# A new order of the same jobs, with fewer changes of the matmul engine's tiling, in an attention-plus-MLP kernel

## Chip, core and metric

The kernel runs on one core of one Trainium2 chip. The metric is the device time of the execution in microseconds; the shown time is the median of three runs. All engines of the core have their own queue of instructions and run them in the order in which they were written; they wait for each other by semaphores. PE is the matmul engine (PEld its loading of the stationary operand), ACT the scalar engine, DVE the vector engine, POOL the general one, SP the queue that issues most transfers.

## The reference

x is 2048 tokens of width 512. It is normalised once (xn), and three terms are added:

```
xn  = layernorm(x)
out = x + attention(xn) + mlp(xn)

attention: 32 heads of 16, 4 segments of 512 tokens
  q, k, v = xn @ wq, xn @ wk, xn @ wv
  per segment s and head:
    p     = softmax(q k^T * scale + causal mask);  a_dot = p v
    a_mem = phi(q) M / (phi(q) z + 1e-6)           phi(t) = t+1 if t>0 else exp(t)
    o     = g * a_mem + (1-g) * a_dot              g = sigmoid(beta)
    M    += phi(k)^T v ;  z += sum phi(k)
  o @ wo
mlp: y = layernorm(xn);  gelu(y @ w1 + b1) @ w2 + b2,  w1 is 512 x 1792
```

## The kernel before

Every weight and activation is carried as a high and a low float16 half, so that each product is three float16 matmuls (line 480, function split3). The work is cut into 1307 small jobs. A *unit* i (0 to 15) is one segment with 8 heads; j (0 to 15) is one half of the MLP's hidden width for 256 tokens.

| job | what it does | PE line, matmuls of one job | tiling of the PE array |
|---|---|---|---|
| T, V | project q, k (T) and v (V) | L480, 12 of 512 columns | whole (128 x 128) |
| D | first MLP product | L480, 12 of 256 columns | whole |
| out | output projection | L815, 12 of 512 | whole |
| warm | 8 matmuls whose result nobody reads | L828 | whole |
| M | logits for the row maximum | L621, 2 or 4 | two row halves (64 x 128) |
| R | turns the 32 row maxima, which go to DRAM (L641) and back (L644) as two more rows of qst | L499, 2 | row halves |
| S | logits again, transposed, with the maximum taken off; ACT makes the exponential (L666), POOL zeroes the masked part (L675) | L661, 2 or 4 | row halves |
| e | second MLP product | L797, 6 | row halves |
| Xt, N, Qd, ratio | turns and the memory's product | L499, L571, L427 | row halves |
| pv | p v and the sum of p for four heads | L690, 8 a block | four column strips (128 x 32) |
| K | memory update | L602 | column strips |

Others have no matmul: G and H are the gelu and its split (L763, L770 to L772, ACT and POOL), O makes the normalised output of a unit (L714, L540, L541, L545, L546, L720 to L726), Q the memory's quotient, X the layer norm, wl, wm and ws load a weight, square it (L311) and split it (L366 to L371); wf (L343, L345) sums the squares on PE for the scale with which a weight is split.

The order in which the jobs are written is a string, ORDER: each letter takes the next job of one of 28 streams (function streams), and a job issues its instructions on all engines at once, so the string sets every engine's order, and that of SP's transfers. A second string, BANKS, names the one of the eight PSUM banks for each call of dense() in that order. There is no scheduler behind it. For the table of ACT functions, plan() adds a load where gelu and exponential follow each other.

The PE array is used as one whole, as two halves by rows, or as four strips by columns. A *change of tiling* is a place in PE's order where a matmul of one kind follows one of another.

Of the kernel before, what the change touches and what calls it, by code (L numbers as in the profile page):

```python
# [56 lines left out]
def streams():  # L57
# [42 lines left out]


ORDER = (
    "aatcucuccvavtctveecttcetcuvaactvuvtaatcattavdtubcwwvccfwxxcxwxyxyxxgyhxcoxxvwxofooowcvwzyzoiyyiazgyyziiynzoiiys"
    "ppAnziiniicvzvcniiooAzmAihiiopzqqiqcivpqjpqjijqqijizqjiqqjiiAwszBzoAskkkkmjiAojoijsoAijAqjqjasAfoAopgkkkkpjpjqq"
    "jlpoolojjjooilihAAkkkkpaiqqiqijqjqqijqjiqjqjisBfgpiiqkkkkmpliqqiooiqpBlqoBopohijjiojiijpolsjiqaqajqiqiqqiiqapka"
    "kmkktspaqijqiqjqiqajqbqajopijjgBfopkkkBkjjjlooooBlhjjjolqiqqiipkkkkjiqqijqqjjiqiqjjqiqiqiBkkkkmpliilfnplimpngrr"
    "mrjjponijqjqjinjipiskmkkmkaiijrijjoojiqsjqqjiqiiiqqkkkkihlqlfmlogojqjqjqqjjasoojmkkkkmqjiqjqjjaojjpipmooisikkkk"
    "lpilhiofmgoooqiqpppqiqiqqqiiiqqpsosmoiqqiiqiqppsslooijqjojijojijoiaakkkkmpaijqjqjaqqqjiqqjiqjqiikmkkakbqiaqqahl"
    "olfqjjojqmjgjjoolmmkkkkmhjjoojjiitjiojiippkkkkliiilnfnimpligniinipmrrijjrsijqjqiqjiqjqiipkmkkksiqjqijqjqjiqjqii"
    "qjqikmpkkkiprlqsphlfojmjgopjjlojpjoomokmkkkqiqisjojiqisjqiqijqqijqhiqqiiqjsqiiqppmkkkkilalofomqpgopaoooospmlajq"  # L110
    "qqjqqjqjqiiqiqqqjqiqqipipooooiijooppoiaakkkkmajiqpisqqjiqjqjaiqaqhjqqqjqaaqmkkkkbjlfoljqjmjgojjqolmkkkkmmjjjooj"
    "jioijoiiippkpkkkiinliifniiilnnimlgrpmjjrmjjjrrijikkpskkiqqijqiqijqqjiqjiqjqiqjiqiispqkpkskksqilqoplfojmjgjjjpoo"
    "oojolmkkkkiqjiqpsjiqiqijqjqiqijqjiqiqiqiiqqkksmkpikplolfjjqmjgjjjoooooklpkmkkjiiopjqiqijqjiqpjqiqijqiqqiqiiqikk"
    "pspkkqiplpoooopljjjqqqjqjjqooolkpskmkpkmqqqpqjpjqqqjqjqpqqjqjqqqkmkkkqlllqqqqqqqqqrrrr"
)

BANKS = (
    "012345670123457063571265407321640573216405732164053271640527163054271630542713605427105472105427105472105472015"  # L120
    "470251407251405712470512470512470536124075631254076340125637123756123576132576132576132576132576135402761350427"
    "163054273106542736574326574326537425632754632574631072456310724563071245360712453620731620731067203617621073621"
    "073621073621037621037621037261702361475023671540263701524603175246031746013746013713460713471630471630463714067"
    "314056723410523674105236741052367410527410527410527410527410527140352671450326475103264751023674523674523647253"
    "647236547236475264735264107532410765324107265431067512043675120436751204736152047361520473615270346150312750317"
    "250317253107250371257013275027135027134650132754062751340621375460376054370567403056374065374065307645307645307"
    "642153076241076241076241076253410762534621075346210754316024310264310432610432610324610324612403246013752640163"
    "754207156437120564371205647312056473120564731206547321065473265104723607423460273460273642073642073642051736420"
    "157642031765420316750316705315631705630157630157630157306173504621357462017345620147536210436024136024316403216"
    "403216403216403216740536740536740536740536271406"  # L130
)


# [777 lines left out]
```

## Time and profile before

| | |
|---|---|
| median of 3 runs | 694.83 us (694.37 to 696.42) |
| profiled execution | span 693.1 us from first to last instruction; what lies around it is 1.7 us by the median, as no time of its own is listed for it |
| PE | 678.7 us busy, 98% of the span, 6359 matmuls |
| DVE, ACT, POOL | 535.4 (77%), 522.7 (75%), 347.2 us (50%) |
| PE idle before matmuls, by releaser | 9.5 us in all, of which 0.2 us between 35 and 680 us |
| transfers | 55.12 MB, mean 80 GB/s |

Matmuls are pipelined, and the recorded end of one is modelled and overlaps the next, so PE's busy time is no measure of useful work. The chain of waits and the distance from one start to the next tell more: a piece of the chain is the time by which the end moves on. PEld's idle time is marked "issue" where it waits for nothing that the profile shows.

### The profile page before, as it was taken

The numbers are of one execution on the slowest core, as the hardware profiler recorded it, in microseconds if no ns is written. First come the engines' busy times: TensorE is split into PE (matmuls) and PEld (weight loads), VectorE is DVE, ScalarE is ACT, GpSimd is POOL, SyncE is SP. The second block draws the span as 40 slices with busy tenths as digits, with TensorE's granted clock in tenths as the row PEclk, the third lists the DMA queues.
The fourth block names the chain that finished last, engine by engine and source line by source line (L and its number), as shares of the span: only waits on it lengthen the run. The fifth ranks groups of instructions, "written<-read, shape, count | busy, mean of one in ns | idle before, by whom it ended". The sixth has DMA issues, their size and how long they took to land.

```text
span 693.1 us, 16949 instructions
## 1 busy us (share of the span) xinstructions
PE 678.7 (98%) x6359; PEld 395.7 (57%) x6359; DVE 535.4 (77%) x1695; ACT 522.7 (75%) x1013; POOL 347.2 (50%) x533
## 2 busy tenths in 40 slices
PE   7799999999999999999999999999999999999997
PEld 6465556576654555566554456567564456656653
DVE  4499978897795887998798786888678595969442
ACT  5989898878795659857795697757795687778870
POOL 5276768365624425664334445454362546455752
PEclk9899999999999999999999999999999999999999
DMA  9984222420204213431113224231120416140101
GB/s 272 283 238 136 64 63 63 108 62 14 84 10 115 87 44 74 100 71 33 51 45 92 63 72 99 63 93 33 31 80 24 132 18 152 18 108 3 18 1 61
DMA packets 51790, 55.12 MB, mean 80 GB/s; under 512 B 4782, under 2 KB 40636, under 8 KB 51708
## 3 DMA queue, kind: packets, MB, share of 16 engines
q1 hardware_dynamic: 49404, 49.84, 25.3%
q0 software_dynamic: 2304, 4.20, 3.7%
q8 instruction: 50, 0.82, 0.5%
q14 instruction: 32, 0.26, 0.1%
HBM read 36.99 MB, written 17.04 MB: 78 GB/s over the span
## 4 chain that ended last, share of the span: by engine, by line
PE 78%; ACT 10%; POOL 4%; DVE 3%; issue 2%; DMA 1%; SPq 1%; POOLq 0%; ACTq 0%; DVEq 0%
PE ps L480 33%; PE ps L797 16%; PE ps L690 10%; PE ps L815 6%; PE ps L661 5%; PE ps L621 5%; ACT pt L666 2%; DVE ps L628 2%; PE ps L571 2%; PE ps L499 1%; ACT hT L763 1%; ACT hT L771 1%; SPq L252 1%; POOL w1s L371 1%; DMA pt<-in_A_wk_dram 1%
## 5 line engine op out<-in xcount | busy, mean ns | idle before, releaser
L628 DVE CUSTOM_DVE_ANT_0 ps<-ps,mask 128x512 f32<-128x512 f32 (+3 forms) x512 | 233.8, 522 | 16.1 <-PE ps L621 14.9
L666 ACT ACTIVATE pt<-ps,qkcs 128x512 f32<-128x512 f32 (+1 forms) x384 | 206.1, 624 | 35.3 <-PE ps L661 33.5
L797 PE MATMUL ps<-w2s,hT 64*128 64x512 f16 x1344 | 176.7, 376 | 0.2
L480 PE MATMUL ps<-xnT,w1s 128*128 128x256 f16 x1344 | 157.8, 273 | 0.0
L675 POOL TENSOR_SCALAR_AFFINE_SELECT pt<-pt 128x256 f32<-128x256 f32 x256 | 99.1, 414 | 92.0 <-ACT pt L666 91.0
L480 PEld LDWEIGHTS <-w1s 128*128 128x128 f16 x1344 | 127.3, 98 | 29.1 <-issue 11.3
L772 POOL TENSOR_TENSOR hT<-hh,hT 128x512 f16<-128x512 f32 x64 | 67.8, 1059 | 82.8 <-ACT hT L771 81.0
L797 PEld LDWEIGHTS <-hT 64*128 64x128 f16 x1344 | 76.3, 94 | 50.7 <-issue 6.0
L690 PE MATMUL ps<-pt,vt 128*32 128x512 f32 (+3 forms) x1024 | 77.3, 435 | 0.1
L756 DVE SCALAR_TENSOR_TENSOR hT<-ps,sc,sr 128x256 f32<-128x256 f32 x112 | 52.1, 478 | 27.2 <-PE ps L480 27.0
L628 DVE DVE_READ_ACCUMULATOR2_ANT mc<- 128x1 f32 x512 | 70.6, 138 | 0.0
L661 PE MATMUL ps<-qst,kst 50*128 50x512 f16 (+3 forms) x512 | 67.5, 298 | 0.3 <-ACT pt L666 0.2
L621 PE MATMUL ps<-kst,qst 48*128 48x256 f16 (+3 forms) x512 | 67.1, 297 | 0.5
L771 ACT ACTIVATE hT<-hh 128x512 f16<-128x512 f32 x64 | 36.6, 572 | 33.4 <-POOL hh L770 32.9
L690 PEld LDWEIGHTS ps<-pt,vt 128*32 128x32 f32 x1024 | 31.3, 109 | 42.4 <-issue 30.8
L770 POOL TENSOR_SCALAR hh<-hT,sc 128x512 f32<-128x512 f32 x64 | 41.8, 653 | 26.6 <-ACT hT L763 24.9
L720 POOL TENSOR_TENSOR nN<-nN,oT 128x512 f32<-128x512 f32 x16 | 20.3, 1267 | 61.3 <-DVE oT L546 61.3
L763 ACT ACTIVATE hT<-hT,b1t 128x256 f32<-128x256 f32 x112 | 46.4, 495 | 0.2
L480 PE MATMUL ps<-xnT,wqs 128*128 128x512 f16 x192 | 45.6, 389 | 0.0
L480 PE MATMUL ps<-xnT,wks 128*128 128x512 f16 x192 | 44.3, 379 | 0.0
L480 PE MATMUL ps<-wvs,xnT 128*128 128x512 f16 x192 | 44.0, 380 | 0.1
L815 PE MATMUL ps<-wos,oT 128*128 128x512 f16 x192 | 43.2, 380 | 0.6 <-POOL oT L726 0.6
(217 smaller groups left out, 890.0 us busy)
## 6 DMA issues: line engine op xcount, KB each, us to landing
kd<-hl SPq DMA_DIRECT2D x48, 128.0 KB
qd<-hl SPq DMA_DIRECT2D x48, 128.0 KB
kst<-kd SPq DMA_DIRECT2D x32, 192.0 KB
qst<-qd SPq DMA_DIRECT2D x32, 192.0 KB
acc<-in_A_x_dram SPq DMA_DIRECT2D x16, 256.0 KB
acc<-in_B_b_dram POOLq DMA_DIRECT2D x16, 256.0 KB, 4.1
out_dram<-acc SPq DMA_DIRECT2D x16, 256.0 KB
xt<-in_A_x_dram SPq DMA_DIRECT2D x14, 256.0 KB
```

Source lines behind the costliest of these rows:

```text
L480: T.matmul(p, wsl(ws, k, a), xsl(xs, k, b), start=s0 and i == 0, stop=s1 and i == 3 * n - 1)
L621: T.matmul(p[:, o:o + n], stk[i, 0][r, t, P * qb:P * qb + P], stk[i, 1][r, t, :n], start=True, stop=True)
L628: V.tensor_tensor_reduce(p[:, o:o + n], p[:, o:o + n], mask[:, 512 - n:], 1.0, -3e38, OP.add, OP.max, mc[:, 16 * b + 4 * t + qb:16 * b + 4 ...
L661: T.matmul(p[:, o:o + n], stk[i, 1][r, t, P * kb:P * kb + P], stk[i, 0][r, t, P * kb:], start=True, stop=True)
L666: A.activation(e[:, OFF[kbs[0]]:OFF[kbs[0]] + o], p[:, :o], AF.Exp, scale=qkcs[:, 1, i % NG:i % NG + 1])
L675: G.affine_select(v, v, pattern=[[0, 2], [1, P]], compare_op=OP.is_ge, fill=0.0, base=0, channel_multiplier=-1)
L690: T.matmul(p[32 * c:32 * c + 32, P * kb:], vt[s, kb][:, 4 * g + c, 16 * odd:16 * odd + 32], pt[i, 2 * c + odd][:, OFF[kb]:OFF[kb] + LEN[kb ...
L756: V.scalar_tensor_tensor(hz[:, fi, :], p[:, :256], col(F1 + fh), srow[hs][:, own], op0=OP.mult, op1=OP.mult)
L763: A.activation(z, z, AF.Gelu_apprx_tanh, bias=b1t[:, FH * (j % 2) + f:FH * (j % 2) + f + 1])
L772: G.tensor_tensor(hT[:, z, 1, :], t, hT[:, z, 0, :], op=OP.subtract)
L797: w = T.matmul(pes[j][a], hTs[fh][r, fi, u, P * a:P * a + P], w2s[r, fo, v, :], start=n == 0 and m == 0, stop=fi == FH - 1 and m == 2, ski ...
L815: T.matmul(p, o[:, u, P * b:P * b + P], wos[:, g, v, :], start=i == 0, stop=i == 3 * NG - 1)
```

## The change

The two strings are replaced. Every stream gives the same jobs in its own order, each job issues the same instructions, and the 32 later loads of ACT's function table stay 32. What differs is how the streams are interleaved, and the bank of each job. In PE's order the whole array is visited 68 times instead of 90, the strips 32 times instead of 34, and the row halves 89 times instead of 110; so there are 189 changes of tiling instead of 234.

```diff
 ORDER = (
-    "aatcucuccvavtctveecttcetcuvaactvuvtaatcattavdtubcwwvccfwxxcxwxyxyxxgyhxcoxxvwxofooowcvwzyzoiyyiazgyyziiynzoiiys"
...
-    "pspkkqiplpoooopljjjqqqjqjjqooolkpskmkpkmqqqpqjpjqqqjqjqpqqjqjqqqkmkkkqlllqqqqqqqqqrrrr"
+    "atttatccauutactavccectuaccvvccuvtvtvevwteavbwawvtucwvwwfxcgxdxhtxcyxccwxvgxsxcfxoxyooxoyyoiiyzynziiyyzitoczoyz"
...
+    "kkkkpqsiplospooqjljqqjqqjljjqooookkkppkqpjqqqpjjqqqqqjjqqjmqkpkkqqmqqqqlqqqqqqllqrrrr"
 )
...
 BANKS = (
-    "012345670123457063571265407321640573216405732164053271640527163054271630542713605427105472105427105472105472015"
...
+    "012345670123457062134570216345270163452071634502751634702516340725163407256134072134207103714203712403174203174"
...
 )
```

**First place: the end of unit 6, PE.** Before, from the fourth product of MLP part 7 (D, L480 with w1s) to its last; ps_n is a PSUM tile. Loads of the stationary operand and repeats of a row are left out.

```order
L480 MATMUL ps_4655<-xnT,w1s 128x256
...
L621 MATMUL ps_4669<-kst_92,qst_90 128x512
...
L661 MATMUL ps_4677<-qst_89,kst_91 128x512
...
L797 MATMUL ps_4413<-w2s,hT_116 128x512
...
L661 MATMUL ps_4691<-qst_89,kst_91 128x384
...
L480 MATMUL ps_4701<-xnT,w1s 128x256
...
L661 MATMUL ps_4715<-qst_89,kst_91 128x256
...
L621 MATMUL ps_4723<-kst_92,qst_90 128x384
...
L480 MATMUL ps_4741<-xnT,w1s 128x256
...
L661 MATMUL ps_4755<-qst_89,kst_91 128x384
...
L480 MATMUL ps_4779<-xnT,w1s 128x256
```

The same jobs now:

```order
L797 MATMUL ps_4456<-w2s,hT_116 128x512
...
L661 MATMUL ps_4713<-qst_89,kst_91 128x512
...
L661 MATMUL ps_4719<-qst_89,kst_91 128x384
...
L480 MATMUL ps_4729<-xnT,w1s 128x256
...
L480 MATMUL ps_4743<-xnT,w1s 128x256
...
L480 MATMUL ps_4757<-xnT,w1s 128x256
...
L480 MATMUL ps_4771<-xnT,w1s 128x256
...
L480 MATMUL ps_4785<-xnT,w1s 128x256
...
L661 MATMUL ps_4799<-qst_89,kst_91 128x256
```

Five products D stand together; before, M, S and e (row halves) stood between them, and the array changed its tiling six times in this stretch, now twice.

**Second place: unit 7's row maxima, PE.** R (L499 with mc) sends the maxima off; S (L661 with qst_90) is the first that needs them back. Before:

```order
L499 MATMUL ps_5087<-ident,mc 96x64
...
L499 MATMUL ps_5098<-ident,xt 128x64
...
L797 MATMUL ps_4894<-w2s,hT_115 128x512
...
L499 MATMUL ps_5124<-ident,xt 128x64
...
L499 MATMUL ps_5139<-ident,phk 128x64
...
L480 MATMUL ps_5155<-xnT,w1s 128x256
...
L480 MATMUL ps_5173<-xnT,wks 128x512
...
L797 MATMUL ps_4894<-w2s,hT_115 128x512
...
L661 MATMUL ps_5204<-qst_90,kst_92 128x512
```

Now:

```order
L499 MATMUL ps_5081<-ident,mc 96x64
...
L427 MATMUL ps_5093<-ident,rat 128x64
...
L797 MATMUL ps_4876<-w2s,hT_115 128x512
...
L661 MATMUL ps_5111<-qst_89,kst_91 128x256
...
L499 MATMUL ps_5119<-ident,xt 128x64
...
L499 MATMUL ps_5133<-ident,xt 128x64
...
L797 MATMUL ps_4876<-w2s,hT_115 128x512
...
L690 MATMUL ps_5155<-pt,vt_85 32x512 x4
...
L661 MATMUL ps_5176<-qst_90,kst_92 128x512
```

A projection and a product D between the two have gone elsewhere, and a block of pv has come in.

**Third place: the start, PE.** From the first projection (wks) to the first product with w1s. Before:

```order
L480 MATMUL ps_393<-xnT,wks 128x512
...
L343 MATMUL ps_416<-am,ones 128x1 x2
L343 MATMUL ps_431<-am,ones 128x1 x2
L345 MATMUL ps_431<-am,ones 128x1
L480 LDWEIGHTS wqs
L480 MATMUL ps_453<-xnT,wqs 128x512
...
L343 MATMUL ps_476<-am,ones 128x1 x2
L499 MATMUL ps_486<-ident,phk 128x64
...
L480 MATMUL ps_504<-xnT,w1s 128x256
```

Now:

```order
L480 MATMUL ps_390<-xnT,wks 128x512
...
L480 MATMUL ps_415<-xnT,wqs 128x512
...
L840 MATMUL ps_439<-ident,mhl 128x14
L499 MATMUL ps_451<-ident,phk 128x64
...
L343 MATMUL ps_472<-am,ones 128x1 x2
L345 MATMUL ps_472<-am,ones 128x1
L480 LDWEIGHTS wqs
L480 MATMUL ps_502<-xnT,wqs 128x512
...
L480 MATMUL ps_529<-xnT,wks 128x512
...
L480 MATMUL ps_559<-xnT,w1s 128x256
```

Unit 0's second projection stands ahead of the sum of w1's squares (ps_431 before, ps_472 now), both projections of unit 1 stand ahead of the first product with w1s, and the sum for w2 (ps_476) has gone behind four such products. On ACT and SP the jobs of the start follow the same new string.

More of the change, by code (lines that the diff above doesn't have):

```diff
@@ L102 @@
 ORDER = (
-    "aatcucuccvavtctveecttcetcuvaactvuvtaatcattavdtubcwwvccfwxxcxwxyxyxxgyhxcoxxvwxofooowcvwzyzoiyyiazgyyziiynzoiiys"
[L104 to L112, printed above, removed]
@@ L113 @@
-    "oojolmkkkkiqjiqpsjiqiqijqjqiqijqjiqiqiqiiqqkksmkpikplolfjjqmjgjjjoooooklpkmkkjiiopjqiqijqjiqpjqiqijqiqqiqiiqikk"
-    "pspkkqiplpoooopljjjqqqjqjjqooolkpskmkpkmqqqpqjpjqqqjqjqpqqjqjqqqkmkkkqlllqqqqqqqqqrrrr"
+    "atttatccauautactavccectuaccvvccuvtvtvevwteavbwawvtucwvwwfxcgxdxhtxcyxccwxvgxsxcfxoxyooxoyyoiiyzynziiyyzitoczoyz"
+    "ypiiisznniwipzAiizozApsnooiiAApqiqiocAcviqivjqpqsjqjqjqijqiqjqBziimzkkkBkisqjzqijoijqhjAoijAAjAfgAoopkskpkkjpBl"
+    "pjloooooAojqjaiAqsiqjqqjlpiqiimkkkkiiqjqqjijqqjiqjhqajqifgopiikkpkmkaiholotplosjijojijpoijioaaqpliaqjqipqpiqiqa"
@@ new lines @@
+    "qkkmkkqajqiqijqijqaqbiqpajBoijjfBBgpomkkBakkjjljooloohjilqiqjiqqjiqipikBkkkijqqijqqjiqiiqjqjqiqjmikkkklomfljjjg"
+    "nlpnannjijriijkkkmpkpijirjisapirrjimqjqjqiiqjqsiikpskkkhlliqqmlofgjqqjqqjqjqqjjommkkkkjiioojijojijosojipimkkkpk"
+    "oloilhimfoogooospipiqpiqqilqsmqqqiiqqiiopoijqipqjqiqjiqpspjjooooojpiakkkkmqisaqjiaqqhjaqamiqjqjqjqiqqqibqjaaqkk"
+    "kkjjlljofjmjgojklkmkkmjjoojjjooijikkppkkiiinlpomipiinnlihilmiifpgprrpimrnjpiqiqjqiqjiqjjrjikkpkkmiiqjisqjqiqjiq"
+    "ijqjqiqhmqjikkkkllsafmjjgopmosoloooojjqijqqjqiimkkkkjmiqqiqshqijiqjqijqjqiiqjqiikkppkkolpolfimpgopoomoojjlqqaqj"
@@ L115 @@
+    "qjqiasqqijqipsqipqqjpiqqipqioooooooiapakkkaksmijqjaajqqiqjqqjqjiqsbqiaaqikkmkklfljqqjqqjmjjgojklkkkjjjoooomhijj"
+    "ooiijkpkmkkiliipnmniippiniliiflnmigmrrjsjjrjjqiqqjiiqmqikkkpkijqqijqijqijqjqiqjsiqipikkpkkqirlplfmjjgoooomjmjjo"
+    "ooilijkkkpkijqipqqjiqsjqjiqiqjiqiqjqipiqikkkkpqilossplfqjmqpgoljjosjjjookkmkkjpjmioijojiqijqijpqiqiqqiiqpiqqiqi"
+    "kkkkpqsiplospooqjljqqjqqjljjqooookkkppkqpjqqqpjjqqqqqjjqqjmqkpkkkqqmqqqqlqqqqqqllqrrrr"
 )
 BANKS = (
-    "012345670123457063571265407321640573216405732164053271640527163054271630542713605427105472105427105472105472015"
@@ L121 @@
[L121 to L130, printed above, removed]
+    "012345670123457062134570216345270163452071634502751634702516340725163407256134072134207103714203712403174203174"
@@ new lines @@
+    "230174203170432157064321570643215706342157630157613057163057160537610537160751360751342607513426730541267304512"
+    "763041527630145276307652307652305726350735260375261740523461705234671056273410562374256374256374256347235467325"
+    "462573426571304265710426357014263750142016375204175632017456302173402713247013240173240127401237405162374052136"
+    "740532617405236147052361470523614705236147052367052367052367053267052367052145213647052136475036475306475347534"
+    "076534076534076213450762145360275314602715346027315426703154267103542671035647210356472103564721305172305172305"
@@ new lines @@
+    "173205132705312573015273027153207153624071254073612540736125346125346125314261543261452365124356132540761325407"
+    "613254076312546315241653241624160752341607523416075342160342136402136241036241036214036271536420736154250734612"
+    "507613245074561327045613270456132047561320475613204756132041732041732041372041307420713402713402713456027156023"
+    "471560234761502135476210365210356231506231503612503612503612503472560134725360147021543670251647356145673145673"
+    "145673145673145670312470371240371240371240536712"
```

## Prediction

> **What bounds the kernel now.** I read the page's busy shares first, then who waited for whom on PE, then stretches of the span, then the chain of waits.
>
> ```profile
> span 693.1 us, 16949 instructions
> PE 678.7 (98%) x6359; PEld 395.7 (57%) x6359; DVE 535.4 (77%) x1695; ACT 522.7 (75%) x1013; POOL 347.2 (50%) x533
> ...
> PE ps L343 <- ACT w1s L311: 4.5, 2, 3.3
> PE ps L828 <- POOL ones L171: 1.6, 1, 1.6
> PE ps L326 <- ACT wqs L311: 1.3, 1, 1.3
> PE ps L466 <- POOL xt L413: 1.0, 1, 1.0
> PE ps L815 <- POOL oT L726: 0.6, 1, 0.6
> PE ps L343 <- ACT w2s L311: 0.3, 1, 0.3
> PE ps L661 <- ACT pt L666: 0.2, 1, 0.2
> ```
>
> PE's idle time is 9.5 us in all, nearly all of it at the start; one 0.6 stands at the end, and between them 0.2. So PE's own stream sets the end. The other engines (stretches: us, then busy time of PE, PEld, DVE, ACT, POOL, then PE's clock):
>
> ```profile
> 20.00:25.00 5.00, 2.59 (x14) 1.44 (x12) 2.89 (x15) 4.94 (x10) 1.80 (x2) 0.97 1.10 345
> 25.00:30.00 5.00, 2.82 (x10) 1.91 (x11) 2.04 (x9) 4.75 (x10) 0.12 (x1) 0.50 1.11 343
> 30.00:35.00 5.00, 4.69 (x32) 2.82 (x31) 1.07 (x3) 4.97 (x10) 2.98 (x4) 0.84 0.46 137
> 40.00:90.00 50.00, 49.50 (x469) 29.26 (x468) 47.35 (x173) 44.74 (x89) 34.30 (x44) 1.00 0.48 136
> 90.00:660.00 570.00, 569.47 (x5463) 330.29 (x5463) 456.56 (x1440) 433.98 (x837) 283.42 (x441) 1.00 0.25 65
> ```
>
> Before 35 us ACT is the full engine, from 40 to 90 DVE and ACT are almost as full as PE, and from 90 on PE alone is: DVE has 113 of 570 us free, ACT 136. A saving on PE is worth its full size there, as long as the others hand over in time.
>
> **What a change of tiling costs.** The chain of waits in order of time (start, how far the end moved on, what):
>
> ```profile
> 303.38 2.73 PE ps L480 x24
> 306.11 0.32 PE ps L621 x2
> 306.43 0.22 PE ps L661 x2
> 306.65 0.65 PE ps L797 x6
> 307.52 1.42 PE ps L480 x12
> 313.93 2.29 PE ps L690 x32
> 345.44 0.48 PE ps L602 x32
> 345.92 2.15 PE ps L690 x32
> 580.38 5.35 PE ps L480 x48
> 615.05 6.66 PE ps L480 x60
> ```
>
> These L480 pieces are products D. Twelve cost 1.42, 24 cost 2.73, 48 cost 5.35, 60 cost 6.66: 1.31 for each dozen and 0.11 once, for coming from the row halves into the whole array. Back again: two 512-column matmuls on the row halves cost 0.32 right behind a D and 0.22 behind their like, so 0.10. Into the strips: 32 matmuls of pv cost 2.29 when they are first there, 2.15 when a memory update (L602) has gone in ahead of them, so 0.14. I take 0.10 for each change, with 0.09 and 0.14 as bounds.
>
> ```profile
> PEld L480 <- issue: 22.8, 77, 0.8
> ```
>
> This row shows why: the load ahead of an L480 stood idle 77 times for 22.8 us with no semaphore to wait for, 0.3 each, about as often as PE enters the whole array (90 visits). Within a run the load lies under the matmul before it; at a change it doesn't. [...]
>
> **The terms.** (1) 234 to 189 is 45 changes: 45 x 0.10 = **-4.5 us** (bounds 45 x 0.09 = -4.0 and 45 x 0.14 = -6.3). Nearly all lie behind 35 us, where no other engine covers them. The matmuls, the ACT table loads and all DVE, ACT and POOL work are the same in number and size.
>
> (2) The start. PE (start, busy, group, idle before it) and one row of ACT:
>
> ```profile
> 1.59 6.69 PE L828 MATMUL ps<-ones 128*128 128x256 f16 x48 [1.59 <-POOL ones L171]
> 28.64 4.18 PE L480 MATMUL ps<-xnT,wqs 128*128 128x512 f16 x12
> 33.25 0.38 PE L343 MATMUL ps<-am,ones 128*128 128x1 f32 x2 [0.31 <-ACT w2s L311]
> 33.96 2.79 PE L480 MATMUL ps<-xnT,w1s 128*128 128x256 f16 x24
> ...
> 30.90 0.61 ACT L370 ACTIVATE w1s<-w1s 128x512 f16<-128x512 f32 x1
> ```
>
> Today the sum of w1's squares holds PE until 28.64 us, and the projection behind it takes 4.18 us at half clock. The new order does that projection first, but puts about six more pieces like the 0.61 of ACT (four splits, two copies of projections) ahead of those squares. So the sum ends 3.6 us later, near 32.3; two projections of 2.6 follow (12 matmuls of 0.22, as the 37 in 8.16 under (4)), and the first w1s product starts near 37.7. What is "level"? Ahead of that product two projections are added (5.2) and the w2 sum is taken away (0.6), one change fewer: 33.96 + 4.5 = 38.5. I take 0 for the start, between -1.5 and, for one more stretch of half clock (6.8 us of it above, which lose 3.4), +3.4.
>
> (3) Hand-overs. Fewer visits mean longer runs, and with the same jobs some pairs stand closer. The closest and longest way is from R to S, through DRAM (chain, unit 13):
>
> ```profile
> 570.33 1.40 DMA md<-mhl
> ...
> 571.75 0.27 SPq L644
> 572.06 3.46 DMA qst<-md
> ...
> PEld L661 <- DMA qst<-md: 0.8, 2, 0.4
> PEld ps L690 <- POOL pt L675: 3.1, 11, 0.5
> ```
>
> That is 5.1 us from the write's issue to the read's landing, after ACT and DVE have emptied the turned maxima. Adding up PE's work between R and S in both orders (a D 1.31, an e 0.65, a pv block 2.18, and so on): under 5.5 us there are three units before and eight now; unit 7 falls from 6.8 to 4.5. It waited twice for 0.4 before. Between the last masked block and its pv less than 2.3 us of PE's work stand 4 times before, 10 times now; such loads waited 11 times for 0.28 each, though mostly under PE's own work. I take **+1.0** (2 of the waits of 0.4 more, and a little for pv), from 0 to +5.0: eight waits of 0.4 are 3.2, six of 0.3 are 1.8. The banks I put at nothing: the shortest way from a bank's last write to its next is 0.3 us of PE's work before and 0.4 now.
>
> (4) The end.
>
> ```profile
> 671.15 6.89 PE L797 MATMUL ps<-w2s,hT 64*128 64x512 f16 x60
> 677.97 2.61 PE L815 MATMUL ps<-wos,oT 128*128 128x512 f16 x11
> 681.20 8.16 PE L815 MATMUL ps<-wos,oT 128*128 128x512 f16 x37 [0.63 <-POOL oT L726]
> ...
> 671.02 0.69 DVE L546 SCALAR_TENSOR_TENSOR rc<-rc,rt 128x512 f32<-128x512 f32 x1
> 673.07 0.72 DVE L714 STREAM_SHUFFLE oT<-nD 128x512 f32<-128x512 f32 x1
> ```
>
> The last pv ends at 671.15, the twelfth matmul of the output projection can start at 681.20: 10.05 us, which ten e (6.5) and eleven matmuls (2.4) cover but for 0.85, from 680.35. Now 13 e cover 8.5 + 2.4 = 10.9, but two DVE instructions of the memory's quotient (0.69 each) have gone in ahead of the shuffle: 11.4. A shortfall of 0.5 is left: **-0.3**.
>
> Sum: -4.5 + 0 + 1.0 - 0.3 = -3.8. On the profiled execution the span goes from 693.1 to 689.3; what lies around it (1.7) doesn't change, so the median goes from 694.83 to **691.0 us**. A measurement of this kernel tells a change from none from about 0.3% on, 2.1 us: faster is under 692.7, slower over 696.9.
>
> **The rivals.**
>
> *The gain is handed back (about 695).* PE waits where it had 0.2 us of waits: the upper bound of (3), 5.0 in place of 1.0, gives 695.0. For it: the eight short ways from R to S, and from 40 to 90 us DVE with 2.65 of 50 us to spare, so that a block that comes late stays late. Against it: the shortest way from R to S was 4.4 us before (unit 14) and is 4.5 now, so no unit is asked for more than one was. [...]
>
> *The start loses the clock (slower, 697.8).* Now the first six warm-up jobs (the 48 matmuls of the L828 row) still end at 8.3 us; the first turn of x then waits for POOL's normalised tile, near 11 us, and the next sum waits for six squares on ACT, to about 17.5. Before, 2.59 us of work in 20 to 25 were too little, and the clock went to 0.50. If that happens twice, around 11 us and again around 25, with the projections in it, 2 x 3.4 = 6.8 us are lost: 691.0 + 6.8 = 697.8. It decides at the first w1s product: with the 4.5 us of changes still to be saved behind it, the whole is level when it starts at 43, and slower by 2.1 past 45. Against it: each of these gaps is near 2.7 us by my estimate from the pieces of ACT and POOL, where before two waits of 4.5 together, the longer 3.3, came close behind each other (the L343 row above), and 43 is 5 us behind what ACT's pieces give. [...]
>
> *Everything falls well (689).* No added hand-over waits, and the start gains 1: 691.0 - 1.0 - 1.0 = 689.0. For it: ACT's pieces put the first w1s product 0.8 ahead of level, and 113 of DVE's 570 us behind 90 us are free.
>
> **How the numbers follow.** Forecast 0.54, everything well 0.12, handed back or half price 0.24, slow start 0.10. Faster by over 0.3%: 0.54 + 0.12 = 0.66; within: 0.24; slower: 0.10. The range goes from 688.8 (all well) to 695.0 (handed back); it leaves out the slow start and the edges, about 2 in 10.
>
> **What would show it.** Right: in the chain D pieces still at 1.31 a dozen plus 0.11; PE's waits between 35 and 680 us under 1.5 us; the first w1s product between 36 and 40 us. Wrong: (1), if pieces on the row halves cost more than now where they aren't behind a change; (2), if that product starts past 41, or the clock row shows under 1.00 after 15 us for longer than before; (3), if PE's wait for qst, or its loads' for pt, grows by more than 2 us; (4), if PE idles over 1 us ahead of the last output projection. Past 694 the forecast is wrong, and past 697 its sign.

## The result and the profile after

The new order takes 721.5 us (median of 4 runs, 718.9 to 722.7) against 694.9 us of the old one measured beside it: 1.0375 times the time, 95% interval 1.035 to 1.040. It is 26.5 us slower; the forecast was 3.8 us faster, and the range ended at 695.0. The profiled execution is the shortest of the four (718.9 us, span 717.2), so its profile shows 24.1 us of the 26.5. Intervals leave out single executions in a slower state, of which two stand far off (860.9 us with short row maxima in the new order, 2413.3 us with everything left out).

The page of the new order; its last row is the share of each engine in the chain of waits:

```profile
span 717.2 us, 16987 instructions
PE 684.1 (95%) x6359; PEld 399.2 (56%) x6359; DVE 542.6 (76%) x1695; ACT 524.6 (73%) x1014; POOL 351.0 (49%) x533
...
PE 53%; DVE 15%; DMA 14%; ACT 11%; issue 4%; POOL 2%; SPq 1%; DVEq 0%; ACTq 0%; POOLq 0%
```

The work is the same, instruction for instruction, but for one load of ACT's function table more (1.28 us at 61.2 us, ahead of L851), so the later loads are 33 and not 32. Only 53% of the chain is PE's now; it was 78% before. DVE needs 542.6 us for the 1695 instructions that took 535.4. PE's waits between 35 and 680 us (total, times, longest), where there were 0.2 us before:

```profile
PE ps L661 <- DMA qst<-md: 6.9, 6, 3.4
PE ps L621 <- DMA qst<-qd: 4.2, 8, 0.9
PE ps L797 <- DVE hT L756: 1.7, 2, 1.3
PE ps L621 <- DVE mc L628: 1.2, 2, 0.8
PE ps L499 <- DVE mc L628: 1.1, 1, 1.1
PE ps L480 <- DVE w1s L367: 0.9, 1, 0.9
```

The two longest are the trips through DRAM: the maxima (md) and q (qd) that come back into qst. In the other four a matmul waits for a bank or an operand that DVE hands over late. They are spread over the run; the stretches that the prediction used (us, busy time of PE, PEld, DVE, ACT, POOL, PE's clock, DMA):

```profile
40.00:90.00 50.00, 46.52 (x429) 27.79 (x429) 45.93 (x167) 44.12 (x86) 33.04 (x40) 1.00 0.58 158
90.00:660.00 570.00, 552.96 (x5256) 321.43 (x5257) 449.11 (x1410) 417.79 (x806) 272.36 (x424) 0.99 0.24 64
396.90:403.70 6.80, 6.21 (x35) 3.00 (x37) 3.05 (x13) 3.05 (x5) 1.64 (x3) 0.50 0.13 42
```

From 90 to 660 us PE had 0.5 us without work before, and has 17.0 now. The last row is a stretch of half clock in the middle of the run, which the old order doesn't have.

How the delays of several queues add up can be followed at unit 8. The rows are of timelines (start, busy, what, idle time before) of POOL, DVE, PE, ACT and SP, with two pieces of the chain of waits (PE's x24, DMA) and one row of SP's waits:

```profile
374.18 1.16 POOL L772 TENSOR_TENSOR hT<-hh,hT 128x512 f16<-128x512 f32 x1 [0.74 <-ACT hT L771]
...
374.24 1.64 DVE L545 TENSOR_TENSOR oT<-oT,nD 128x512 f32<-128x512 f32 x1
...
377.07 0.65 PE L621 MATMUL ps<-kst,qst 48*128 48x384 f16 x5 [0.82 <-DVE mc L628]
378.10 0.38 PE L480 MATMUL ps<-xnT,wks 128*128 128x512 f16 x1 [0.38 <-DVE mc L628]
...
378.10 5.35 PE ps L480 x24
...
385.96 2.90 ACT L763 ACTIVATE hT<-hT,b1t 128x256 f32<-128x256 f32 x7
...
389.52 0.34 DVE L639 SCALAR_TENSOR_TENSOR mhl<-ps,mhl 32x64 f16<-32x64 f32 x2
392.22 0.69 DVE L545 TENSOR_TENSOR rc<-rc,rt 128x512 f32<-128x512 f32 x1 [2.36 <-ACT rt L541]
...
SPq L527 <- DMA qd<-hl: 1.7, 1, 1.7
...
390.71 0.79 SPq L527 DMA_DIRECT2D qst<-qd x2
391.56 0.91 SPq L737 DMA_DIRECT2D out_dram<-acc  x2
392.51 0.46 SPq L641 DMA_DIRECT2D md<-mhl  x1
...
392.51 3.40 DMA md<-mhl
...
397.49 1.02 PE L661 MATMUL ps<-qst,kst 50*128 50x512 f16 x2 [3.39 <-DMA qst<-md]
```

A product of DVE (L545) that lasts 0.69 us at 392.22 takes 1.64, beginning while POOL's L772 runs. The row maxima behind it end 0.95 late, so M and the two projections T of unit 9 start late on PE (0.82 and 0.38). Behind the projections, ACT has seven gelu pieces to do, and only then come unit 8's maxima; DVE has them ready at 389.86. On SP, unit 9's q must land first (1.7 us of waiting) and is fetched again (L527), and two rows of the output leave (L737), before the maxima's write is issued at 392.51, 2.65 us after they were ready. The write, issued behind these transfers, takes 3.40 us; it took 1.40 in unit 13 of the old order. PE stands still for 3.39 us, and its clock is at 0.50 for 6.8 us from 396.87 on, which by estimate costs another 3.1 (half of the 6.2 us that PE is busy in that stretch).

### The profile page after: what moved, and what is told of

Same layout as the page of the kernel before. It is cut to its first block, busy times and chain, and to the rows that moved or that the text cites. A ratio compares the mean times of both kernels' runs of the same rounds, so it can differ in the third digit from the quotient of the medians.

```text
span 717.2 us, 16987 instructions
## 1 busy us (share of the span) xinstructions
PE 684.1 (95%) x6359; PEld 399.2 (56%) x6359; DVE 542.6 (76%) x1695; ACT 524.6 (73%) x1014; POOL 351.0 (49%) x533
## 4 chain that ended last, share of the span: by engine, by line
PE 53%; DVE 15%; DMA 14%; ACT 11%; issue 4%; POOL 2%; SPq 1%; DVEq 0%; ACTq 0%; POOLq 0%
PE ps L480 16%; PE ps L797 15%; PE ps L690 6%; DVE ps L628 5%; PE ps L661 4%; PE ps L621 4%; PE ps L815 4%; DMA qd<-hl 4%; DMA qst<-qd 3%; DMA md<-mhl 2%; ACT hT L763 2%; DMA qst<-md 1%; ACT pt L666 1%; DVE hl L518 1%; DVE mc L628 1%
## 5 line engine op out<-in xcount | busy, mean ns | idle before, releaser
L628 DVE CUSTOM_DVE_ANT_0 ps<-ps,mask 128x512 f32<-128x512 f32 (+3 forms) x512 | 234.8, 522 | 18.7 <-PE ps L621 15.6
L797 PE MATMUL ps<-w2s,hT 64*128 64x512 f16 x1344 | 182.8, 379 | 1.8 <-DVE hT L756 1.7
L675 POOL TENSOR_SCALAR_AFFINE_SELECT pt<-pt 128x256 f32<-128x256 f32 x256 | 101.8, 422 | 116.3 <-ACT pt L666 115.2
L480 PE MATMUL ps<-xnT,w1s 128*128 128x256 f16 x1344 | 155.9, 273 | 1.3 <-DVE w1s L367 0.9
L480 PEld LDWEIGHTS <-w1s 128*128 128x128 f16 x1344 | 128.8, 98 | 27.5 <-issue 8.2
L797 PEld LDWEIGHTS <-hT 64*128 64x128 f16 x1344 | 78.7, 95 | 55.9 <-issue 8.2
L772 POOL TENSOR_TENSOR hT<-hh,hT 128x512 f16<-128x512 f32 x64 | 66.8, 1044 | 80.5 <-ACT hT L771 77.0
L621 PE MATMUL ps<-kst,qst 48*128 48x384 f16 (+3 forms) x512 | 74.2, 300 | 6.5 <-DMA qst<-qd 4.2
L661 PE MATMUL ps<-qst,kst 50*128 50x512 f16 (+3 forms) x512 | 72.6, 299 | 8.0 <-DMA qst<-md 6.9
L756 DVE SCALAR_TENSOR_TENSOR hT<-ps,sc,sr 128x256 f32<-128x256 f32 x112 | 51.3, 477 | 30.4 <-PE ps L480 30.3
L628 DVE DVE_READ_ACCUMULATOR2_ANT mc<- 128x1 f32 x512 | 71.3, 139 | 0.2
L661 PEld LDWEIGHTS <-kst 50*128 50x128 f16 x512 | 29.3, 95 | 38.7 <-issue 11.9
L621 PEld LDWEIGHTS <-qst 48*128 48x128 f16 x512 | 30.5, 95 | 33.9 <-issue 12.9
L480 PE MATMUL ps<-xnT,wks 128*128 128x512 f16 x192 | 45.2, 386 | 0.5 <-DVE mc L628 0.4
L480 PE MATMUL ps<-xnT,wqs 128*128 128x512 f16 x192 | 44.1, 379 | 0.0
```

What stands on the lines that cost most here:

```text
L480: T.matmul(p, wsl(ws, k, a), xsl(xs, k, b), start=s0 and i == 0, stop=s1 and i == 3 * n - 1)
L621: T.matmul(p[:, o:o + n], stk[i, 0][r, t, P * qb:P * qb + P], stk[i, 1][r, t, :n], start=True, stop=True)
L628: V.tensor_tensor_reduce(p[:, o:o + n], p[:, o:o + n], mask[:, 512 - n:], 1.0, -3e38, OP.add, OP.max, mc[:, 16 * b + 4 * t + qb:16 * b + 4 ...
L661: T.matmul(p[:, o:o + n], stk[i, 1][r, t, P * kb:P * kb + P], stk[i, 0][r, t, P * kb:], start=True, stop=True)
L675: G.affine_select(v, v, pattern=[[0, 2], [1, P]], compare_op=OP.is_ge, fill=0.0, base=0, channel_multiplier=-1)
L756: V.scalar_tensor_tensor(hz[:, fi, :], p[:, :256], col(F1 + fh), srow[hs][:, own], op0=OP.mult, op1=OP.mult)
```

## The experiments

The expectations call PE TensorE, DVE VectorE and POOL GpSimd. The first theory was that the trips and SP's one queue make up the loss (A); its rival was that DVE hands the PSUM banks back late where row maxima crowd (B). In runs that leave work out it is said what; line numbers shift by one to four where lines were taken out.

**The trips.** In the first run the maxima don't go to DRAM and back (the two rows of qst that they fill are zero). In the second the fetch (L527) reads the copy of the unit before, so that it waits for no write just issued (the logits are then of other units). The third has both edits, and the fourth has both in the old order.

```diff
+            G.memset(qst[j][64 * b + 32:64 * b + 64].rearrange("p a c -> p (a c)").bitcast(F32), 0.0)
...
-        Q.dma_start(d.rearrange("a p c -> p a c"), hl)
...
-            Q.dma_start(stk[i, 0][64 * b + KM:64 * b + KS], dv[:, 4 * b:4 * b + 4, :])
...
-                d = (qd, kd)[w][i % 2]
+                d = (qd, kd)[w][(i + 1) % 2 if i else 0]
```

> The new order, but the row maxima are not sent to DRAM and back (L641, L644 left out; two rows of qst stay zero, so the maximum is not taken off); R's turn and its ACT and DVE work stay. Theory A (the two round trips through DRAM on SP's queue, q and k, and the maxima, hold PE): PE's loads waited 10.1 us for the maxima in place of 0.8, and the half-clock stretch behind the 3.4 us wait of unit 8 cost 3.4, so 721.5 - 9.3 - 3.4 = 709 (706 to 712). Theory B (lumps of row-maximum work on DVE hold banks and so PE): the maxima's trip is covered by other waits, 717 to 721.

> The new order, but each unit's reads of q and k (L527) take the copy that the unit before has written, so that SP does not wait for this unit's writes to land; the transfers are the same in number and size, unit i computes with q and k of unit i-1. Theory A: the 8.0 us of loads waiting for qst<-qd go, and the write of the maxima is no longer queued behind that wait (part of the 10.1), 721.5 - 8 - 3 = 710 (706 to 714). Theory B: 717 to 721.

> The new order with both edits of the two runs before. Theory A: nearly all of the added time goes; the forecast's 691 plus the DVE waits of some 8 us that the trace of the new order also shows, 699 (694 to 703). Theory B: 715 to 720.

> The old order with the same two edits, the control: its PE waited 0.8 us for the maxima and not at all for q and k, so both theories say 693 to 695. The difference of this run to the one with the new order and both edits is what the order alone is worth without the trips: 45 changes at 0.10 would make the new order 4 us faster.

Measured: 715.4 (ratio 1.029, 1.027 to 1.031), 718.2 (1.029 to 1.038), 712.3 (1.021 to 1.028) and, in the old order, 694.9 (1.000, 0.999 to 1.001). Of the new order's three, 715.4 and 712.3 lie between the ranges of A and B, 718.2 in that of B. Without the trips the new order is 9.2 us faster and the old one no faster; 17.4 are left. So the trips are a third of the loss, or more, since the first edit also puts work in. To make the two rows zero, POOL has four memsets more at the start. From the third run:

```profile
L200 POOL MEMSET qst<- 32x1024 f32 x4 | 3.8, 960 | 0.0
41.58 4.64 PE L481 MATMUL ps<-xnT,w1s 128*128 128x256 f16 x41
```

The split of the first weight on POOL starts at 21.61 us and not at 17.99, and the first w1s product starts at 41.58 us, where the new order with the trips has it at 37.32 (in the old order 35.08 in place of 33.96). By estimate the trips are worth between 9.2 and, if all of this delay reaches the end, 13.5 us.

In the third run the waits for md are gone; what stands between 100 and 680 us (L622 is M, L500 R, L657 S; VectorE's L629 is the row maximum):

```profile
PE ps L622 <- DMA qst<-qd: 1.3, 4, 0.5
PE ps L622 <- DVE mc L629: 1.2, 2, 0.8
PE ps L500 <- DVE mc L629: 1.1, 1, 1.1
PE ps L657 <- DVE mc L629: 0.9, 3, 0.4
```

**The row maxima.** Each row maximum runs over 64 columns of its block; the number of DVE's instructions stays. Once with neither trip, once with the trips, and once in the old order.

```diff
-   V.tensor_tensor_reduce(p[:, o:o + n], p[:, o:o + n], mask[:, 512 - n:], 1.0, -3e38,
+   V.tensor_tensor_reduce(p[:, o:o + 64], p[:, o:o + 64], mask[:, 384:448], 1.0, -3e38,
```

> The new order with neither trip and, beside that, every row maximum (L628) taken over 64 columns of its block in place of all of its 128 to 512: the same number of VectorE instructions, some 140 us less of VectorE's 542 us of work, and a result that is not the reference's. The last run left 17.4 us that the trips do not explain (712.3 against 694.9 for the old order with neither trip). Theory A (VectorE hands the accumulator banks back late where row maxima come in a crowd; TensorE waits for banks): nearly all of the 17.4 goes and the saved changes of tiling show, 690 to 696. Theory B (the matmul stream itself became slower, by the new neighbours on the array or by more changes of clock): nothing moves, 708 to 713.

> The new order with only the row maxima cut to 64 columns, both trips through DRAM left in; not the reference's result. If the two causes add, what is left is the trips' 9 us: 699 to 706. If the trips' waits were only paid because VectorE was late too, it lies below 697; if VectorE has no part in it, 718 to 722.

> The old order with the row maxima over 64 columns (not the reference's computation), both trips left in. With all three covers the old order came to 689.1, 5.8 under its own time, though its TensorE waits between 35 and 680 us are 0.2 in the trace. If VectorE's row maxima are what holds it up in that hidden way: 689 to 691, and of the 10.5 us that the same edit gave the new order only about 5 belong to the new order alone. If it was GpSimd's work: 693.5 to 695, and the new order's 10.5 are its own.

Measured: 701.8 (1.007 to 1.011), 710.5 (1.018 to 1.023), and 693.7 in the old order (0.997 to 0.999). L628 in that last run:

```profile
L628 DVE CUSTOM_DVE_ANT_0 ps<-ps,mask 128x64 f32<-128x64 f32 x512 | 100.6, 253 | 73.6 <-PE ps L621 66.9 <-ACT pt L666 4.8 <-PE ps L661 1.1
```

The edit brings the new order 10.5 us without the trips and 11.0 with them: the two causes add. It brings the old order 1.2, which is in the range given for GpSimd's work as the cause; the rest belongs to the new order. 710.5 itself lies in none of its ranges, as the first took the trips to be all that is left. But 701.8 lies above the 690 to 696 that late banks alone would give, and below the 708 of a slower stream, so a third cause is left.

**The fillers.** The old order's last two warm jobs are left out (a letter t each in ORDER, and its bank).

```diff
-iqqiiqapkakmkktspaqijqiqjqiqa
+iqqiiqapkakmkkspaqijqiqjqiqa
...
-kkkkmhjjoojjiitjiojiippkkkkli
+kkkkmhjjoojjiijiojiippkkkkli
```

> The old order, full computation, without the two filler jobs (L828, eight matmuls of ones that nobody reads) that it holds near 140 and 331 us. The change moved them to the start, where TensorE waits anyway. Each is 0.87 us of matmuls and stands between other kinds of work, so two of them with the changes beside them are 2.0 us: 692.7 if the stream of TensorE sets the end there. If they only fill time in which TensorE would wait anyway, 694 to 695.

Measured 694.9 (1.000, 0.999 to 1.001): nothing for 2.0 us of matmuls. (The times in the expectation are PE's work added up; in the trace the two stand near 158 and 353 us. Nor did the change move both to the start: they are near 49 and 143 us in its trace.) The waits on PE between 100 and 680 us in that run:

```profile
PE ps L621 <- ACT nD L699: 0.8, 1, 0.8
PE ps L661 <- ACT pt L666: 0.4, 1, 0.4
PE ps L621 <- ACT pt L666: 0.2, 1, 0.2
```

Where the fillers stood PE now waits for ACT to empty banks. In the old order's profile this was busy time. Its 98% were thus not a proof that PE alone sets the end.

**GpSimd.** In the trace of the new order the instructions of DVE that are stretched most (L529, L545, L546, L560, L367) have their inputs in SBUF and, stretched, began while POOL ran (L546 lasts 0.69 us, and 1.54 to 1.68 when it began during L772). One run shortens POOL's work at three places, a second puts memsets there that keep POOL busy as long (the diff's last line, L772 alone shown):

```diff
-        G.tensor_tensor(hT[:, z, 1, :], t, hT[:, z, 0, :], op=OP.subtract)
+        G.memset(hT[:, z, 1, :].bitcast(F32), 0.0)
...
+        G.memset(t, 0.0); G.memset(t[:, :, :(190 if n == 2 else 128)], 0.0)
```

> The new order with GpSimd's long tensor-tensor work taken out in three places: the low half of the split of h is set to zero (L772, 64 times 1.06 us become a memset), and two products for the memory (L583, L722, 24 times 1.28 us) do 32 of 512 columns; the result is not the reference's. In the trace of the new order VectorE's instructions with operands in SBUF alone (L529, L545, L546, L560, L367) last up to 1.1 us longer than their like, and each such one began while a GpSimd instruction ran and ended 0.07 to 0.55 us behind that one's end: 20 us in all in the new order and 15 in the old. Replaying the new order's own trace with these instructions at their short durations ends 7.2 us earlier, the old order's 0.4. Theory A (those stretched instructions are a good part of what makes VectorE hand banks back late): 711 to 716. Theory B (GpSimd's work matters only through who waits for its results): 718 to 720. Theory C (neither matters): 721 and over.

> The new order with the same three places of GpSimd's work replaced (L772, L583, L722), but this time with memsets that keep GpSimd busy for about as long as before (1.2 to 1.3 us, of the smaller L772 0.7), so that it hands on as late as in the new order; the result is not the reference's. In the traces so far no VectorE instruction that began during a GpSimd memset was stretched (seven cases, 2 ns at most). If the 9.4 us of the run with short GpSimd work came from VectorE no longer being stretched: 711 to 716. If they came from GpSimd being done earlier: 719 to 722.

Measured 712.1 (1.023 to 1.027) and 717.8 (1.031 to 1.034). The first two rows are from the new order, the others from the run with memsets:

```profile
L772 POOL TENSOR_TENSOR hT<-hh,hT 128x512 f16<-128x512 f32 x48 | 55.9, 1165 | 67.6 <-ACT hT L771 64.1 <-DVE st L390 1.7 <-DMA qd<-hl 1.7
L546 DVE SCALAR_TENSOR_TENSOR oT<-oT,nD 128x512 f32<-128x512 f32 x16 | 14.8, 925 | 0.5
...
L546 DVE SCALAR_TENSOR_TENSOR oT<-oT,nD 128x512 f32<-128x512 f32 x16 | 11.2, 697 | 0.5
L772 POOL MEMSET hh<- 128x512 f32 x48 | 25.5, 530 | 0.0
L772 POOL MEMSET hh<- 128x380 f32 x48 | 20.2, 420 | 2.8
L772 POOL MEMSET hT<- 128x256 f32 x48 | 15.0, 312 | 67.2 <-ACT hT L771 67.2
```

The memsets last 0.53 + 0.42 + 0.31 = 1.26 us, against the 1.17 that they replace, and DVE's L546 is back at 0.70 from 0.93. The first run fell by 9.4 us, as the theory of the stretched instructions had it, but with POOL kept busy by memsets only 3.7 of them are left (with an uncertainty of about 2 by the two intervals); the other 5.7 go to POOL being done earlier. The second run lies between its two expectations: both are at work, and the replay of the trace (7.2 us) had the first too large.

**Everything left out at once**, in both orders: neither trip, short row maxima, short POOL work.

> The new order with everything taken away at once: neither trip through DRAM, row maxima over 64 columns, short GpSimd work. If hand-overs are the whole price of the new order and the 45 saved changes are real, what is left is TensorE's own stream: 692 to 697, the upper part if the clock at the start is at half for longer as in the two earlier runs without trips, and no more than 3 above the old order treated the same way. If the stream itself became slower by its new neighbours, 700 and over, 6 or more above the old order treated the same way.

> The old order with the same work taken away. Its TensorE waits in its trace are 0.2 us between 35 and 680 us, so if these are all that hand-overs cost it: 693 to 695. If the old order too is held up in ways that its busy share hides (the run without the two fillers got nothing for 2.0 us of matmuls saved): 685 to 691.

Measured 695.1 (ratio to the old order as it is 1.000, 0.999 to 1.001) and 689.1 (0.991 to 0.994). The old order falls by 5.8 as well, the second of its two expectations. The new order falls by 26.4, to where it was expected; against the old order treated the same way, 20.5 of the 26.5 us are gone. It is still 6.0 us above that one, not 3 or less. PE's longest waits before 100 us, new order, then old:

```profile
PE ps L344 <- ACT wvs L312: 5.2, 1, 5.2
PE ps L327 <- ACT wqs L312: 2.6, 1, 2.6
...
PE ps L344 <- ACT w1s L312: 4.7, 2, 3.3
PE ps L467 <- POOL xt L414: 1.6, 1, 1.6
```

All rows of these views together are 12.7 and 9.4 us, so 3.3 of the difference stand in the first 100 us. Part of this is the edit's own: with its memsets the first w1s product starts 4.2 us later than in the new order as it is (41.52), in the old order 2.3 later (36.24). Between 100 and 680 the waits are 1.2 and 0.2. The rest of the 6.0, and the 4.5 saved that should have come off it, I can't assign to rows; it stays open, and a stream of PE that is itself slower in the new order, the rival in the expectation, isn't ruled out for it.

| left out | new order | old order |
|---|---|---|
| nothing | 721.5 | 694.9 |
| both trips | 712.3 | 694.9 |
| long row maxima | 710.5 | 693.7 |
| long POOL work at three places | 712.1 | not run |
| trips and row maxima | 701.8 | not run |
| all three | 695.1 | 689.1 |

**Mended versions**, the full computation. The row maximum becomes one plain reduction, in the old order without the late fillers; two products (L720, L583) then go from POOL to DVE as well, in both orders.

```diff
-   V.tensor_tensor_reduce(p[:, o:o + n], p[:, o:o + n], mask[:, 512 - n:], 1.0, -3e38,
-                          OP.add, OP.max, mc[:, 16 * b + 4 * t + qb:16 * b + 4 * t + qb + 1])
+   V.tensor_reduce(mc[:, 16 * b + 4 * t + qb:16 * b + 4 * t + qb + 1], p[:, o:o + n], axis=AX.X, op=OP.max)
...
-            G.tensor_tensor(n, n, r, op=OP.mult)
+            V.tensor_tensor(n, n, r, op=OP.mult)
```

> A full version that the runs point to: the old order without its two late fillers, and with the row maximum taken by one plain reduction in place of a masked one and a read of the accumulator (L628). The maximum then also covers the keys that the mask hides in the diagonal block; it is only subtracted in the exponent and divides out. VectorE's 317 us on this line are to become 512 instructions of some 0.25 to 0.65 us, so about 20 to 90 us less work for it. If VectorE's row maxima hold the old order up: 689 to 693, faster than both kernels. If not, or if a plain reduction over 512 columns takes as long as the pair it replaces: 694 to 696.

> Full computation: the old order without late fillers and with the plain row maximum (693.2 before), and two of GpSimd's products (L720 and L583, 28 times 1.27 us) given to VectorE, where such an instruction takes 0.69. GpSimd loses 36 us, VectorE gains 19. If GpSimd's work holds the old order up (with all three covers it fell by 5.8, with short row maxima alone by 1.2): 689 to 692. If VectorE's later hand-back costs as much as that brings: 693 to 695.

> The same two edits (plain row maximum, L720 and L583 on VectorE) in the new order, full computation. They take away some of what the new order stumbles over, but leave both trips through DRAM and most of VectorE's load: 710 to 717, still slower than the old order. If the new order were only short of a little time on these engines and gained as much as from the work left out: 700 to 709.

Measured: 693.2 us (0.9966 to 0.9984), 698.0 (1.003 to 1.005) and 715.7 (1.029 to 1.033). The first beats both kernels, by 0.25% of the old order. DVE's row for 512 columns in it:

```profile
L628 DVE TENSOR_REDUCE mc<-ps 128x1 f32<-128x512 f32 x128 | 82.1, 682 | 15.6 <-PE ps L621 14.9
```

It replaces a pair of 0.72 and 0.14, which overlap in part; DVE's busy time falls by 22 us to 513.6. Giving DVE 28 products more costs 4.8 us, though POOL's busy time falls by 29.8 (36 were expected): the forecast of 689 to 692 for it had the wrong sign, and the other, 693 to 695, was too low. As far as this run shows, the old order has no room for more on DVE where those products stand. The new order's 715.7 is in the first of its two ranges.

## Why the prediction was wrong

**What bounds the kernel: the reading was wrong.** The prediction took 98% busy and 0.2 us of waits as proof that PE's stream sets the end, so that a saving there "is worth its full size, as long as the others hand over in time". The run without the fillers saved 2.0 us on PE and gained 0.0; with all three kinds of work left out the old order fell by 5.8, though PE's matmuls stayed the same. PE in that run:

```profile
PE 675.4 (98%) x6359; PEld 386.7 (56%) x6359; DVE 406.7 (59%) x1695; ACT 522.4 (76%) x1013; POOL 279.3 (41%) x537
```

The same 6359 matmuls are busy for 675.4 us, 3.3 less than before: this points to waiting that the profile counts as busy. A matmul of 512 columns is recorded as 0.38 us long, while the next starts 0.22 behind it (12 in 2.6), so by this a wait under 0.16 us shows in no row. "113 of 570 us free" on DVE was an average over a queue that works in order.

**Term (1), the changes: right in size where it can be read, and not seen in the time.** D pieces of the new order's chain:

```profile
72.94 1.42 PE ps L480 x12
269.58 2.73 PE ps L480 x24
528.26 5.35 PE ps L480 x48
313.34 6.66 PE ps L480 x60
```

They are the same to 0.01 us as before: 1.31 a dozen and 0.11 once. The loads ahead of an L480 stand idle less often, as fewer visits should have it:

```profile
PEld L480 <- issue: 15.7, 59, 0.8
```

That is 18 fewer than the 77 before, and 7.1 us less than the 22.8. These rows are of the way into the whole array alone, about half of the 45 changes. That the 4.5 us are saved and spent on waiting is likely, but not shown: PE's busy time rose by 5.4 us, and with everything left out the new order is still 6.0 behind. The half price, which shares the chance of 0.24 with the gain handed back, was an assumption: no run shows how the 0.10 divides, and the D pieces show 0.11 in both orders.

**Term (2), the start, was right.** The first w1s product was to start between 36 and 40, by estimate at 37.7:

```profile
20.91 0.38 PE L343 MATMUL ps<-am,ones 128*128 128x1 f32 x2 [1.98 <-ACT wvs L311]
37.32 5.40 PE L480 MATMUL ps<-xnT,w1s 128*128 128x256 f16 x48
```

It starts at 37.32. The rival in which the start loses the clock came in part; PE's clock is the third number from the right:

```profile
20.00:25.00 5.00, 4.09 (x16) 2.21 (x17) 3.16 (x7) 4.97 (x11) 1.98 (x3) 0.66 0.88 285
25.00:30.00 5.00, 4.55 (x28) 2.15 (x26) 3.69 (x6) 3.91 (x7) 0.57 (x1) 1.00 0.17 52
```

It is 0.66 for 5 us and then full; before it was 0.50 from 25 to 30 and 0.84 from 30 to 35. Both gaps of the rival are there, 2.63 us up to 16.23 and 1.98 up to 20.91. Behind the second the clock was at 0.50 for 3.4 us, from 21.4 on, which by estimate costs 1.7 (half of it) and not 6.8. That both gaps would be shorter than the 3.3 us before was no argument against the rival: the longer one left the clock at 1.00, and the half clock came behind the shorter one. In the old order the clock fell at 24.73, when PE had stood still for 2.10 of its 3.31 us (its matmuls ended at 22.63). That only one of the two gaps cost clock was luck as far as the prediction goes. More was lost in the middle of the run, where no rival looked.

**Term (3), the hand-overs, is the step that failed.** It was put at +1.0 with +5.0 as the upper bound. PE's waits between 35 and 680 us came to 20.2 us in the profiled execution, all rows of that view added up, with 3.1 of lost clock beside them. With the 4.5 that the changes should save and the 1.2 by which the first w1s product came ahead of level (37.32 against 38.5), that is 17.6 of the 24.1. Each wait costs more than the idle time listed, by the 0.16 us above: by estimate 4.6 for the 29 waits, and under 2 us stay open. The bound was wrong in three ways. First, it counted eight units with less than 5.5 us of PE's work between R and S and priced each at 0.4, what a wait had cost before; it took for granted that R's own inputs are on time and that SP is free. At unit 8 neither held, and one wait cost 3.4 and about as much again in clock (3.1). That T's fetches and R's write share SP's queue stood in the order, and the prediction did not price it; the trips are 9.2 us or more. Second, "the banks I put at nothing" rested on the shortest way from a bank's last write to its next, 0.3 against 0.4 us of PE's work. That number doesn't tell how much work DVE has in front of it when the bank falls due: with short row maxima the new order gains 10.5 to 11.0 us, the old 1.2. Third, all durations were taken as fixed. Some of DVE's instructions last longer when they fall on POOL's (L546 0.69 us or up to 1.68), and what falls on what is changed by a new order; about 3.7 us go back to that, and 5.7 to POOL's results that come late, each give or take 2.

**Term (4), the end, was right.** The new order's last rows on PE:

```profile
694.12 8.83 PE L797 MATMUL ps<-w2s,hT 64*128 64x512 f16 x78
702.88 10.53 PE L815 MATMUL ps<-wos,oT 128*128 128x512 f16 x48
```

The 0.63 us of idle time ahead of the output projection are gone; -0.3 was expected.

**The rivals.** "The gain is handed back" had the mechanism: a block that comes late stays late, with the short ways from R to S and the full DVE as its grounds. It was bounded at 695 by the same +5.0 as term (3). What spoke against it, that no unit is asked for more than one was before, compared one distance at a time, while in the run the delays of several queues add up along one chain, as at unit 8.

## What to carry to other kernels

In a kernel as full as this one (PE 98%, DVE 77%, ACT 75% busy), a busy share near 100% on one of them doesn't say what a saving there is worth; leave out a piece of its work and see whether the time follows (here 2.0 us less gave 0.0), and look whether the edit puts other work in, as the memsets did here. An order of jobs is to be judged by how much each in-order queue has in front of it when a result falls due, the transfer queue and its waits for landings included, and with durations that may grow (here L546's from 0.69 to 1.68 us), not by the distance between two jobs on the busiest engine. Here fewer changes of tiling, at 0.10 us each, weren't worth longer runs of work that another engine must empty.

## What the runs showed of the hardware

- Some DVE instructions with inputs in SBUF lasted longer when they began during a computation of POOL, and ended just behind it. In the new order L546, with two such inputs, lasts 0.69 us by the median; of 28, four began during L772 and lasted 1.54 to 1.68, and one during L675 0.77, all ending 0.54 or 0.55 behind POOL's. L560, 0.22 by the median, lasted 0.43 to 1.22 in eight of 48, ending 0.07 to 0.09 behind (six others that began so kept 0.21 to 0.24), and L529, 0.48 by the median, 0.85 to 1.40 in eight of 24, ending 0.28 behind (five others kept 0.47 or 0.48). L756, which reads PSUM, kept its length: of 112, 61 began during a computation of POOL, and the longest lasted 0.49 us against 0.48 by the median. In the run with memsets L546 (oT) is at 0.70 us in the mean, from 0.93; L529 is at 0.57 (phq) and 0.69 (phk), from 0.71 and 0.72.
- PE's clock fell to 0.50 in or behind some of its idle times. In the middle of the new order, where PE stands still for 3.39 us from 394.10 on, it is 0.50 for 6.8 us from 396.87 on; the price, by estimate another 3.1 us, is nearly as large as the wait. At the new order's start it is 0.50 for 3.4 us from 21.40 on, behind an idle time of 1.98 us that ended at 20.91, while one of 2.63 us up to 16.23 left it at 1.00. In the old order it is 0.50 for 6.8 us from 24.73 on, within an idle time of 3.31. So in these traces the length of an idle time alone doesn't tell whether the clock falls.
- The write of the 16 KB of maxima took 3.40 us at unit 8 of the new order, issued behind transfers of q and out, and 1.40 in the old order's unit 13.
